# Chunk 3's probabilities transposed by VectorE and twelve transfers, with their values planned 1.5 units behind the scores

## The chip, the core and the metric

The kernel runs on one core of one Trainium2 chip. The metric is the device time of one execution in microseconds; lower is better. The engines that matter are TensorE (PE in the rows: matmuls, and matrix transposes through an identity), VectorE (DVE), ScalarE (ACT), GpSimd (POOL) and SyncE (SP), which here only issues transfers (DMAs). Each engine works through its own list of instructions in order.

## The reference

Two stages: windowed attention (8 batches, 8 heads, 576 positions, head size 64), then a feed-forward block on 4608 tokens of width 512.

```python
def _attn_ref(q, k, v):
    scores = scale * np.matmul(q, k.transpose(0, 1, 3, 2))
    mask = (rel >= 0) & (rel < 64)          # rel = query position - key position
    scores = np.where(mask, scores, -1e9)
    attn = np.exp(scores - np.max(scores, axis=-1, keepdims=True))
    attn = attn / (np.sum(attn, axis=-1, keepdims=True) + 1e-09)
    return np.matmul(attn, v)

def _moe_ref(x, w_in, w_out):
    h = x @ w_in                             # 512 -> 2048
    sp = np.where(h > 20.0, h, np.log1p(np.exp(np.minimum(h, 20.0))))
    return (h * np.tanh(sp)) @ w_out         # 2048 -> 512
```

## The kernel before

The 4608 tokens are cut into 12 chunks of 384. For each chunk the attention gives `x` (as a high part `xh` and a low part `xl`), and the feed-forward block then runs over 16 blocks `f` of the hidden width. One step of it is `ffn_in` (12 matmuls into `h_ps`; L223 to L238 then work on the result with VectorE, ScalarE and GpSimd) and `flush` (9 matmuls into the three accumulators `acc`, of the step two back). In the rows a step of the steady state is therefore twelve `h_ps` matmuls and nine `acc` matmuls.

The attention of a chunk is done in 4 pairs of heads (`p` = 0 to 3), while the feed-forward block of the chunk before it runs: chunk 3's attention lies inside chunk 2's feed-forward block. A pair has three parts. `scores` is 24 small matmuls into `s_ps`; then six reductions (L150), six exponentials (L153) and the normalisation (L161 to L163) give the probabilities `pr`; the loads of `q_t` and `k_t` for the pair two later follow on SP. `transpose` turns `pr` into `pT`. `values` is 24 small matmuls into `o_ps` (from `pT` and `v_t`), the copies to `xh` and `xl` (L205, L206), and on SP the load of `v_t` for the pair two later, which waits until this pair's values are through TensorE, since there are two buffers.

`transpose` exists in two forms. Up to chunk 3: six TensorE transposes into PSUM tiles `t_ps` (L184), then two copies from there into `pT` (L185, one on ScalarE, one on VectorE). From chunk 4 on: one VectorE transpose of 32x32 blocks into `tr` (L173), then twelve transfers of 24 KB (L178), all issued by SP, which put the blocks at their places in `pT`. The first matmul of `values` waits for all twelve. I call the twelve a train below. `tr` takes its buffers from the same two that `pr` uses.

What runs when is planned in half-steps, called slots here: slot 2n follows the n-th `ffn_in`, slot 2n+1 the n-th `flush`. `plan` (L320) places pair p's scores at begin + p·step, its transpose 0.6·step later, its values lag·step later, with lag 1. For chunk 3, begin is 71 and the last values fall on 90, so that step is 19/4 = 4.75 slots; from chunk 4 on a step is 8 slots. A scheduler then orders VectorE's and ScalarE's instructions by its own estimate of times and by priorities; TensorE's order within the attention follows the plan.

Of the kernel before, what the change touches and what calls it, by code (L numbers as in the profile page):

```python
# [27 lines left out]
def tile_window_attn_mish_ffn(  # L28
# [11 lines left out]
    NPAIR, _, NT = qT.shape  # L40
# [65 lines left out]
    def bank(c, p, name):  # L106
        if c == 2 or (c == 0 and p % 2 == 0):
            return ps_acc.tile([P, CH], F32, name=name, tag=next(sums))
        return ps_at.tile([P, CH], F32, name=name, tag="at")
# [55 lines left out]

    def att_transpose(c, p, pr):
        pT = next(pTs)
        if c > 3:


            moved = []
            tr = ap_.tile([P, P // 32, HM, 32], F32, name="tr", tag="pr", bufs=2)
            nc.vector.transpose(tr.rearrange("p k j i -> p j k i"),  # L173
                                pr.rearrange("p j (k i) -> p j k i", i=32))
            for r in range(0, P, 32):
                for k in range(0, P, 32):
                    if 0 <= k - r % BLK <= BLK:
                        moved.append(nc.sync.dma_start(pT[k:k + 32, r // 32, :, :], tr[r:r + 32, k // 32, :, :]))  # L178
            return pT, moved
        for h in range(2):  # L180
            t_ps = (bank(c, p, "t_ps") if c else ps_h.tile([P, CH], F32, name="t_ps", tag="h_ps")
                    ).rearrange("p (m k) -> p m k", k=P)
            for m in range(NM):
                order.append(nc.tensor.transpose(t_ps[:, m, :], pr[:, h * NM + m, :], ident).ins)  # L184
            (nc.scalar.copy if h == 0 else nc.vector.tensor_copy)(  # L185
                pT[:, :, h * NM:(h + 1) * NM, :].rearrange("p r m i -> p m r i"),
                t_ps.rearrange("p m (r i) -> p m r i", i=32))
        return pT, []
# [101 lines left out]
    class Att:  # L290
# [18 lines left out]
        def transpose(self, p):  # L309
            with in_order():  # L310
                self.pT[p] = att_transpose(self.c, p, self.pr.pop(p))
# [55 lines left out]
    starts = {c: 2 * len(steps) + 2 * NF * (c - 2) for c in range(2, NCHUNK)}  # L367
    steps += [(c, f) for c in range(2, NCHUNK) for f in range(NF)]

    atts = [Att(c) for c in range(NCHUNK)]  # L370
# [20 lines left out]
    ahead = 6  # L391
    begin = starts[2] + ahead + 1
    for c in range(3, NCHUNK):
        atts[c].plan(begin, (starts[c] - ahead - begin) / NPAIR)
        begin = starts[c] - ahead
    events.sort(key=lambda e: e[:2])
    ordered.append(True)
# [52 lines left out]
```

## Time and profile before

| | us |
|---|---|
| median of 3 runs (964.61 to 969.32) | 967.43 |
| the profiled execution | 967.45 |
| its span, first to last instruction | 965.6 |
| TensorE busy | 918.2 |
| VectorE busy | 489.0 |
| ScalarE busy | 624.5 |
| GpSimd busy | 330.4 |

The profiled execution's time is 1.85 us above its span, and within 0.1 us of the median. The rows of the next sections come from that execution; times in them are microseconds from the start of its span. The timeline gives the start of an instruction and its duration, merges equal neighbours (x24), and shows in brackets how long its engine had been idle before and what ended that. The chain of waits that ended last gives, in order of time, which work the end of the kernel hung on.

### The profile page before, as it was taken

What the parts mean: (1) busy time and instruction counts of PE and PEld (TensorE: products, weight loads), DVE (VectorE), ACT (ScalarE), POOL (GpSimd) and SP (SyncE); (2) the same over time, 40 slices, a digit from 0 to 9 for tenths busy, and PEclk for the clock granted to TensorE, in tenths of its full rate; (3) what the DMA queues carried; (4) which work ended last, traced back from release to release, by engine and by line L of the source; (5) the groups of instructions that cost most, each with busy time, mean ns of one, the idle gap of its engine ahead of it and who ended that gap; (6) DMA issues with size and microseconds to landing.
All of it is one profiled execution on the core that took longest, in us unless ns stands there. A gap on an engine that the chain in (4) does not pass through costs nothing.

```text
span 965.6 us, 18005 instructions
## 1 busy us (share of the span) xinstructions
PE 918.2 (95%) x6432; PEld 813.7 (84%) x6432; DVE 489.0 (51%) x1352; ACT 624.5 (65%) x1529; POOL 330.4 (34%) x419
## 2 busy tenths in 40 slices
PE   4667989999999999999999999999999999999997
PEld 3556878888888888888988898889888898889996
DVE  6799884353455445545444544544454544452222
ACT  5677676675666666666666665766756666665664
POOL 2253554223323333233333333333323333333333
PEclk9679999999999999999999999999999999999999
DMA  7645430131123223222222311311312322200000
GB/s 247 193 165 192 136 107 1 51 98 55 52 70 102 65 54 85 80 57 78 85 56 63 100 54 54 114 52 54 114 51 56 104 59 56 89 24 13 33 1 34
DMA packets 80345, 76.16 MB, mean 79 GB/s; under 512 B 9600, under 2 KB 71552, under 8 KB 80256
## 3 DMA queue, kind: packets, MB, share of 16 engines
q1 hardware_dynamic: 80256, 75.01, 25.5%
q8 instruction: 51, 0.84, 0.4%
q14 instruction: 38, 0.31, 0.1%
HBM read 56.10 MB, written 9.44 MB: 68 GB/s over the span
## 4 chain that ended last, share of the span: by engine, by line
PE 83%; DVE 6%; issue 3%; ACT 3%; DMA 3%; POOL 1%; SPq 1%; ACTq 0%; POOLq 0%; DVEq 0%
PE h_ps L96 38%; PE acc L96 37%; PE o_ps L96 4%; PE s_ps L96 3%; DMA st<-w_out 2%; DVE wa L277 1%; DVE wa L278 1%; ACT wa L273 1%; SPq L178 1%; POOL wo_l L280 1%; ACT pr L153 1%; DVE wi_l L280 1%; PE t_ps L184 1%; DVE pr L150 0%; DVE wa L276 0%
## 5 line engine op out<-in xcount | busy, mean ns | idle before, releaser
L224 ACT ACTIVATE t<-t 128x384 f32<-128x384 f32 x192 | 100.7, 524 | 266.1 <-DVE t L223 265.7
L237 POOL TENSOR_SCALAR gh<-t 128x384 fp32r<-128x384 f32 x176 | 91.3, 519 | 518.1 <-DVE t L233 498.3
L96 PE MATMUL h_ps<-xh,wi_h 128*128 128x384 f32 x768 | 261.6, 341 | 3.3 <-DVE t L233 3.2
L96 PE MATMUL h_ps<-xh,wi_l 128*128 128x384 f32 x768 | 259.4, 338 | 0.0
L96 PE MATMUL h_ps<-xl,wi_h 128*128 128x384 f32 x768 | 259.2, 337 | 0.0
L96 PE MATMUL acc<-wo_h,gh 128*128 128x512 f32 x576 | 231.0, 401 | 0.5 <-POOL gh L237 0.5
L96 PE MATMUL acc<-wo_l,gh 128*128 128x512 f32 x576 | 226.6, 393 | 0.0
L233 DVE SCALAR_TENSOR_TENSOR t<-t,h_ps 128x384 f32<-128x384 f32 x176 | 97.3, 553 | 245.6 <-ACT t L231 240.7
L238 POOL TENSOR_TENSOR gl<-t,gh 128x384 fp32r<-128x384 f32 x192 | 199.0, 1036 | 38.6 <-ACT gh L235 24.0
L96 PE MATMUL acc<-wo_h,gl 128*128 128x512 f32 x576 | 205.5, 393 | 0.0
L96 PEld LDWEIGHTS h_ps<-xh,wi_h 128*128 128x128 f32 x768 | 145.3, 189 | 13.5 <-DVE t L233 5.4
L96 PEld LDWEIGHTS h_ps<-xl,wi_h 128*128 128x128 f32 x768 | 145.3, 189 | 6.7
L96 PEld LDWEIGHTS h_ps<-xh,wi_l 128*128 128x128 f32 x768 | 145.4, 189 | 0.0
L223 DVE TENSOR_SCALAR t<-h_ps 128x384 f32<-128x384 f32 x192 | 106.5, 555 | 68.3 <-PE h_ps L96 64.8
L96 PEld LDWEIGHTS acc<-wo_h,gh 128*128 128x128 f32 x576 | 109.0, 189 | 24.1 <-issue 6.5
L96 PEld LDWEIGHTS acc<-wo_h,gl 128*128 128x128 f32 x576 | 108.7, 189 | 23.7 <-POOL gl L238 0.7
L96 PEld LDWEIGHTS acc<-wo_l,gh 128*128 128x128 f32 x576 | 109.0, 189 | 16.7 <-issue 0.2
L230 ACT ACTIVATE t<-t,half_b 128x384 f32<-128x384 f32 x192 | 118.3, 616 | 5.6
L229 ACT ACTIVATE t<-t,one_b 128x384 f32<-128x384 f32 x192 | 118.4, 616 | 4.2
L153 ACT ACTIVATE pr<-pr,mx 128x128 f32<-128x128 f32 x288 | 111.4, 389 | 8.5 <-DVE mx L150 8.5
L231 ACT ACTIVATE t<-t 128x384 f32<-128x384 f32 x192 | 100.2, 522 | 4.6
L150 DVE CUSTOM_DVE_ANT_0 pr<-s_ps,mask 128x128 f32<-128x128 f32 x288 | 64.4, 285 | 7.5 <-PE s_ps L96 7.5
(49 smaller groups left out, 668.1 us busy)
## 6 DMA issues: line engine op xcount, KB each, us to landing
v_t<-vN SPq DMA_DIRECT2D x48, 384.0 KB, 3.7
k_t<-kT SPq DMA_DIRECT2D x47, 224.0 KB, 3.8
out<-o SPq DMA_DIRECT2D x36, 256.0 KB, 2.3
pT<-tr SPq DMA_DIRECT2D x384, 24.0 KB, 1.8
q_t<-qT SPq DMA_DIRECT2D x47, 192.0 KB, 3.7
st<-w_in SPq DMA_DIRECT2D x16, 512.0 KB, 4.0
st<-w_out SPq DMA_DIRECT2D x16, 512.0 KB, 3.5
q_t<-qT SPq DMA_DIRECT2D x3, 64.0 KB, 2.0
```

What stands on the lines that cost most here:

```text
L96: order.append(nc.tensor.matmul(*args, **kw).ins)
L150: nc.vector.tensor_tensor_reduce(out=pr[:, j, :], in0=s_ps[h][:, m, :], in1=mk, op0=ALU.add, op1=ALU.min, scale=-0.125, scalar=3.0e38, acc ...
L153: nc.scalar.activation(pr[:, j, :], pr[:, j, :], AF.Exp, bias=mx[:, j:j + 1], scale=-1.0, accum_out=sm[:, j:j + 1])
L223: nc.vector.tensor_scalar(t, h_ps, 20.0, None, ALU.min)
L224: nc.scalar.activation(t, t, AF.Exp)
L229: nc.scalar.activation(t, t, AF.Square, bias=one_b)
L230: nc.scalar.activation(t, t, AF.Ln, bias=half_b, scale=0.5)
L231: nc.scalar.activation(t, t, AF.Exp, scale=-1.0)
L233: nc.vector.scalar_tensor_tensor(t, t, -1.0, h, ALU.add, ALU.mult)
L237: nc.gpsimd.tensor_scalar(gh, t, 1.0, 0.0, ALU.mult, ALU.add)
L238: nc.gpsimd.tensor_tensor(gl, t, gh.bitcast(F32), ALU.subtract)
L280: (nc.vector if first else nc.gpsimd).tensor_tensor(wl, af, wh.bitcast(F32), ALU.subtract)
```

## The change

Chunk 3 takes the second form of `transpose`. Its plan gets 1.5 units between scores and values, and the unit becomes 19/4.5 = 4.22 slots, so that the last values still fall on slot 90.

```diff
     def att_transpose(c, p, pr):
         pT = next(pTs)
-        if c > 3:
+        if c > 2:
...
     for c in range(3, NCHUNK):
-        atts[c].plan(begin, (starts[c] - ahead - begin) / NPAIR)
+        if c == 3:
+
+            atts[c].plan(begin, (starts[c] - ahead - begin) / (NPAIR + 0.5), lag=1.5)
+        else:
+            atts[c].plan(begin, (starts[c] - ahead - begin) / NPAIR)
         begin = starts[c] - ahead
```

Outside chunk 3's attention the order of instructions is the same on each engine, but for the place of one or two `acc` matmuls among their neighbours. Inside it, three things move.

On TensorE, at chunk 3's first pair, the values leave their place beside the second pair's scores (numbers behind names, as in `pT_106`, are buffers):

```order
@@ -831,5 +830,4 @@
 L96 MATMUL h_ps<-xl_1974,wi_h 128x384
 L96 MATMUL h_ps<-xh_1973,wi_l 128x384
-L96 MATMUL o_ps<-pT_106,v_t 64x64 x12
 L96 MATMUL s_ps<-k_t,q_t 64x128 x12
 L96 MATMUL acc_2376<-wo_h,gh 128x512
```

and come one step later, after the next twelve `h_ps` matmuls:

```order
@@ -854,4 +852,5 @@
 L96 MATMUL h_ps<-xl_1974,wi_h 128x384
 L96 MATMUL h_ps<-xh_1973,wi_l 128x384
+L96 MATMUL o_ps<-pT_106,v_t 64x64 x12
 L96 MATMUL acc_2376<-wo_h,gh 128x512
 L96 MATMUL acc_2376<-wo_l,gh 128x512
```

The second and third pair go the same way; only the fourth pair's values keep a neighbour, the first scores of chunk 4. With `S`, `V`, `h` and `a` for the scores, the values, twelve `h_ps` and nine `acc` matmuls, the row before was S0 h a h T0 a h V0 S1 a h a T1 h a V1 S2 h a h T2 a h V2 S3 a h a T3 h V3, and is now S0 h a h a h S1 a h V0 a h S2 a h V1 a h S3 a h V2 a h a h V3.

On SP, in chunk 3's attention, the loads stood alone before:

```order
L117 DMA q_t<-qT 128x384
L119 DMA k_t<-kT 128x448
L126 DMA v_t<-vN 128x6x128
L117 DMA q_t<-qT 128x384
L119 DMA k_t<-kT 128x448
L126 DMA v_t<-vN 128x6x128
```

and now have a train between them, the second pair's (into `pT_107`) behind the `v_t` load that waits for the first pair's values:

```order
L178 DMA pT_106<-tr 32x192 x12
L117 DMA q_t<-qT 128x384
L119 DMA k_t<-kT 128x448
L126 DMA v_t<-vN 128x6x128
L178 DMA pT_107<-tr 32x192 x12
L117 DMA q_t<-qT 128x384
L119 DMA k_t<-kT 128x448
```

On VectorE, at the second pair, the copy out of PSUM came behind the normalisation:

```order
L163 TENSOR_TENSOR pr<-pr,sm 128x768
L223 TENSOR_SCALAR t<-h_ps 128x384
L185 COPY pT_107<-t_ps 128x3x4x32
L233 SCALAR_TENSOR_TENSOR t<-t,h_ps 128x384
L223 TENSOR_SCALAR t<-h_ps 128x384
```

and the block transpose now stands two instructions behind it (for the first pair none lies between; for the third and fourth it is the same two):

```order
L161 TENSOR_SCALAR sm<-sm 128x6
L162 RECIPROCAL sm<-sm 128x6
L163 TENSOR_TENSOR pr<-pr,sm 128x768
L233 SCALAR_TENSOR_TENSOR t<-t,h_ps 128x384
L223 TENSOR_SCALAR t<-h_ps 128x384
L173 STREAM_TRANSPOSE tr<-pr 128x6x4x32
```

## Rows read from the trace of the kernel before

**Rows 1.** The page: span, TensorE's busy time, granted clock in 40 slices (tenths).

```profile
span 965.6 us, 18005 instructions
...
PE 918.2 (95%) x6432; PEld 813.7 (84%) x6432; DVE 489.0 (51%) x1352; ACT 624.5 (65%) x1529; POOL 330.4 (34%) x419
...
PEclk9679999999999999999999999999999999999999
```

**Rows 2.** The chain that ended last, chunk 3's attention: start, us, work.

```profile
222.17 0.85 PE o_ps L96 x24
223.01 2.28 PE h_ps L96 x12
...
239.75 0.82 PE s_ps L96 x24
240.56 2.29 PE h_ps L96 x12
242.85 2.05 PE acc L96 x9
244.90 2.08 PE h_ps L96 x12
246.98 0.66 PE t_ps L184 x6
247.64 2.08 PE acc L96 x9
...
251.80 0.85 PE o_ps L96 x24
252.65 0.82 PE s_ps L96 x24
253.46 2.27 PE acc L96 x9
```

**Rows 3.** VectorE's timeline, pair 0 of chunk 3 and pair 1 of chunk 4.

```profile
244.48 0.96 DVE L163 TENSOR_TENSOR pr<-pr,sm 128x768 f32<-128x768 f32 x1
...
314.08 0.55 DVE L223 TENSOR_SCALAR t<-h_ps 128x384 f32<-128x384 f32 x1
314.55 0.97 DVE L173 STREAM_TRANSPOSE tr<-pr 128x768 f32<-128x768 f32 x1
```

**Rows 4.** SP's timeline of transfers issued in chunks 4 and 6, and the page's landing time.

```profile
315.58 7.49 SPq L178 DMA_DIRECT2D pT<-tr  x12
...
326.08 0.39 SPq L126 DMA_DIRECT2D v_t<-vN  x1
...
544.44 0.59 SPq L178 DMA_DIRECT2D pT<-tr  x1
...
573.78 8.76 SPq L178 DMA_DIRECT2D pT<-tr  x12
...
pT<-tr SPq DMA_DIRECT2D x384, 24.0 KB, 1.8
```

**Rows 5.** TensorE's timeline: scores and values of that pair, and values that waited.

```profile
307.56 0.89 PE L96 MATMUL s_ps<-k_t,q_t 64*64 64x128 f32 x24
...
325.12 0.92 PE L96 MATMUL o_ps<-pT,v_t 128*64 128x64 f32 x24
...
546.75 0.92 PE L96 MATMUL o_ps<-pT,v_t 128*64 128x64 f32 x24 [0.60 <-DMA pT<-tr]
```

**Rows 6.** TensorE behind idle stretches; the stage row ends in granted clock, DMA share, GB/s.

```profile
22.37 0.48 PE L96 MATMUL o_ps<-pT,v_t 128*64 128x64 f32 x2 [2.39 <-ACT pT L185]
...
22.00:24.00 2.00, 1.63 (x26) 1.45 (x26) 2.00 (x7) 0.71 (x3) 0.00 (x0) 0.50 0.27 82
...
81.36 0.85 PE L184 MATMUL t_ps<-ident,pr 128*128 128x128 f32 x6 [1.36 <-ACT t L224]
...
96.96 0.78 PE L96 MATMUL acc<-wo_h,gh 128*128 128x512 f32 x1
...
100.85 0.92 PE L96 MATMUL o_ps<-pT,v_t 128*64 128x64 f32 x24
```

## The prediction

> **What bounds the kernel now.** I read the page first. TensorE is busy 918.2 of 965.6 us, no other engine over two thirds, and the granted clock stands at nine tenths or more from the fourth of the forty slices on [rows 1]. Then the chain of waits in the stretch that the change touches, 239 to 293 us: every piece of it is TensorE's, one block after another without a gap [rows 2]. So in this stretch a microsecond of work taken off TensorE is a microsecond of span, and a microsecond that TensorE has to wait is one too. Nothing later gives it back, because the stretch behind is bound in the same way. What VectorE and ScalarE gain or lose counts only where TensorE waits for them.
>
> **What leaves TensorE.** Six transposes take 0.66 us, and the block behind them at most 0.03 more (2.08 against 2.05 for nine `acc`) [rows 2]. Four pairs: 2.7 us less. The copies out of PSUM that go with them lie beside TensorE's work and are worth nothing.
>
> **What comes back on TensorE.** Small matmuls slow the block behind them. Alone, the scores cost 0.82 us and 0.21 on the next block (2.29 against 2.08), 1.03 in all; alone, the values cost 0.85 and 0.20 (2.28 against 2.08), 1.05. Side by side they cost 0.85 + 0.82 + 0.22 (2.27 against 2.05) = 1.89 [rows 2]. Parting them therefore costs 1.03 + 1.05 - 1.89 = 0.19 us, and the new order parts three pairs: 0.6 us. TensorE's own work thus falls by 2.7 - 0.6 = 2.1 us.
>
> **The new wait.** The values now wait for a train, so its length has to be found from the trace. SP needs 7.49 us to issue twelve transfers, 0.62 each, and they land 1.8 us after issue [rows 4]. Values that did wait for a train started 546.75 - 544.44 = 2.31 us after the start of its last issue [rows 4, 5]; the landing time alone would say 1.8. The last issue starts 7.49 - 0.59 = 6.9 us after the first. So values can start 8.7 to 9.2 us after SP begins the train, and I take 9.1, near the values that did wait. From chunk 4 on that fits, but only just: the train of 315.58 is ready at 324.7 and its values start at 325.12, 17.56 us after their scores at 307.56 [rows 4, 5].
>
> From the scores to the end of the VectorE transpose that same pair takes 314.55 + 0.97 - 307.56 = 7.96 us, with one instruction (L223) between normalisation and transpose [rows 3, 5]. In chunk 3 the first pair has none: normalised at 244.48 + 0.96, so transposed at 246.4. Pairs 1 to 3 have two, the second for 0.47 us more (314.08 to 314.55), less something, since VectorE also emptied an accumulator (L261) within that pair's 7.96 us, which it doesn't do here. I take 8.2 us, between 7.6 (pair 0's 6.7 and two instructions) and 8.4.
>
> Now pair by pair, with TensorE's blocks from above and the rest of the order taken as it stands, from the scores at 239.75 on:
> - Pair 0: without T0 the second scores start at 246.98 + 2.05 + 2.08 = 251.1 and the values are due at 251.1 + 1.03 + 2.05 + 2.08 = 256.3. Train ready: 246.4 + 9.1 = 255.5. No wait, 0.8 us to spare.
> - Pair 1: due 256.3 + 1.05 + 2.05 + 2.08 + 1.03 + 2.05 + 2.08 = 266.6. Ready 251.1 + 8.2 + 9.1 = 268.4. **Wait 1.8.**
> - Pair 2: here SP's queue decides. Its train stands behind the `v_t` load, which waits for pair 1's values: in the row of 326.08 that load is issued 0.96 us after the values start and takes 0.39 [rows 4, 5]. So the train begins 1.4 us after 268.4, at 269.8, and is ready at 278.9. Due 268.4 + 10.3 = 278.7. **Wait 0.2.** The transpose itself (done by 270) is not the last here. It also needs `tr` free, which pair 1's train gives back when it has landed, at about 268.1, before the transpose would start at 268.6.
> - Pair 3: its scores start at 268.4 + 1.05 + 2.05 + 2.08 = 273.6, so its train is ready at 273.6 + 8.2 + 9.1 = 290.9. Due, with no scores in between, 278.9 + 1.05 + 2 x (2.05 + 2.08) = 288.2. **Wait 2.7.**
>
> The waits come to 4.7 us. TensorE's list is in order, so the feed-forward block that is queued behind each waiting matmul waits with it; that is why a wait here is lost in full.
>
> **What costs nothing.** The VectorE transpose (0.97 us) in place of a copy is hidden by the same TensorE blocks. It can put off the release of an `h_ps` buffer behind it (L233) by about that much, but each buffer is wanted again only two `ffn_in` later, 2 x (2.05 + 2.08) = 8.3 us after it was begun. Without that cover it would be 0.97 us a pair. The loads of `q_t` and `k_t` that now stand behind a train are wanted ten or more us after they land. The new train of pair 3 is over on SP before the first train of chunk 4 is due.
>
> **Sum.** -2.1 + 4.7 = +2.6 us against the profiled execution's 967.45: 970.1 us, 0.3% more. With 7.6 and 8.7 instead of 8.2 and 9.1 the waits fall by 2.1 (to 0.8, 0 and 1.8), with 8.4 and 9.2 they rise by 0.7. One train as slow as that of 573.78 (8.76 against 7.49 [rows 4]; some 5 of the 32 trains are visibly longer than 7.6) adds 1.3. So this case spans 968 to 972.
>
> **Rivals.**
> (A) *The train is hidden and only the saving shows*: 967.45 - 2.1 = 965.3. This needs trains of at most about 4.8 us (7.49 less the longest wait, 2.7), or transposes that come as much sooner. For it speaks that in later chunks the values hardly ever wait. Against it, that their trains have 17.56 us from scores to values, while pair 1 here has 15.5 and pair 3 has 14.6. Most trains take 7.48 to 7.50. The Trainium skill (DMA: Bandwidth & Descriptors, section Issuing engines are not separate DMA queues) says that the sequencer's time to initiate a transfer is usually small relative to the transfer itself. By that rule a train would be ready little over one landing after its start, which is this rival's time; the trace doesn't agree, with 0.62 us for each issue against 1.8 us to landing, and twelve in a row.
>
> (B) *The wait costs the clock, and the kernel is slower beyond doubt.* After an idle stretch of 2.39 us early in the kernel TensorE worked at a granted clock of 0.50, that is 1.2 GHz; after one of 1.36 us six transposes still took 0.85 us, as at 2.4 GHz [rows 6]. At the low level nine `acc` matmuls took 100.85 - 96.96 = 3.9 us [rows 6] instead of 2.05, 1.8 us lost before the clock came back; with the work around them I count 2.2. Pair 3's wait of 2.7 us is the place, and it decides from somewhere between 1.4 and 2.4 us on. That gives 970.1 + 2.2 = 972.3, and with pair 1's wait as well 974.5. Against it: the early stretch lay among others (the engine was idle much of the time around it), while here TensorE works without a gap on both sides.
>
> **How the numbers follow.** The forecast, waits that outweigh the saving: 0.63. (A): 0.15. (B): 0.20. Something not thought of: 0.02. About 0.5%, 4.8 us, is what a measurement of this kernel can tell from no change: below 962.6 is faster, above 972.3 slower. Faster: even (A) doesn't reach it, 0.03. Slower: most of (B) and a slow train or two, 0.19. Within 0.5%: 0.78. The range goes down to (A), 965.0, and up to (B) with one loss of clock and some more, 973.2; left out are (B) twice over and gains beyond (A).
>
> **What would show it.** In the trace of the changed kernel: no `t_ps` from 240 us on; four trains of about 7.5 us on SP between 246 and 290 us; first pair's values without a wait; idle time of TensorE ended by the transfer to `pT` of about 1.8, 0.2 and 2.7 us before the second, third and fourth values; the fourth at about 291 us; a `v_t` load at the head of the third train; granted clock 1.00 through the stretch. The prediction is wrong if a train of twelve takes markedly less than 7.5 us here, if the transposes come over a microsecond sooner than 8.2 us after the scores, or if the clock falls after pair 3's wait.

## The result and the profile after

The changed kernel takes 970.68 us (median of 16 runs, 968.40 to 974.51) against 967.48 for the kernel before (16 runs): ratio 1.0036, 95% interval 1.0026 to 1.0046. It is slower by 3.2 us, small but clear of zero. The profiled execution took 968.54 us with a span of 966.8, which is among the shortest of the runs; a possible reason for part of the spread comes out below.

The page of the kernel after, against [rows 1]: TensorE has 2.6 us less to do, and yet the span is 1.2 us longer.

```profile
span 966.8 us, 18025 instructions
...
PE 915.6 (95%) x6408; PEld 809.9 (84%) x6408; DVE 489.0 (51%) x1352; ACT 623.4 (64%) x1525; POOL 331.6 (34%) x419
...
PEclk9779999999999999999999999999999999999999
```

TensorE's timeline in chunk 3's attention, its scores and values alone (start, us, work; idle time before it and what ended it in brackets):

```profile
238.77 0.89 PE L96 MATMUL s_ps<-k_t,q_t 64*64 64x128 f32 x24
250.14 0.89 PE L96 MATMUL s_ps<-k_t,q_t 64*64 64x128 f32 x24
255.32 0.92 PE L96 MATMUL o_ps<-pT,v_t 128*64 128x64 f32 x24
260.52 0.89 PE L96 MATMUL s_ps<-k_t,q_t 64*64 64x128 f32 x24
267.05 0.92 PE L96 MATMUL o_ps<-pT,v_t 128*64 128x64 f32 x24 [1.27 <-DMA pT<-tr]
272.24 0.89 PE L96 MATMUL s_ps<-k_t,q_t 64*64 64x128 f32 x24
278.39 0.92 PE L96 MATMUL o_ps<-pT,v_t 128*64 128x64 f32 x24 [0.90 <-DMA pT<-tr]
...
289.47 0.92 PE L96 MATMUL o_ps<-pT,v_t 128*64 128x64 f32 x24 [1.69 <-DMA pT<-tr]
```

The first pair's values start without a wait; those of pairs 1, 2 and 3 wait for the transfer into `pT`, 3.9 us in all. The chain of [rows 2], which was TensorE's alone, now runs through SP's issues here and, from the last issue of each of these trains, through its landing (start, us, what):

```profile
265.12 1.84 DMA pT<-tr
...
276.46 1.79 DMA pT<-tr
...
287.39 1.80 DMA pT<-tr
```

A last transfer lands 1.8 us after its issue began, as in the kernel before [rows 4], and the values start 0.1 to 0.3 us after that. SP's trains in the same stretch, and the load between them:

```profile
245.61 8.05 SPq L178 DMA_DIRECT2D pT<-tr  x12
...
258.22 7.48 SPq L178 DMA_DIRECT2D pT<-tr  x12
...
267.99 0.38 SPq L126 DMA_DIRECT2D v_t<-vN  x1
268.56 8.49 SPq L178 DMA_DIRECT2D pT<-tr  x12
...
280.27 7.71 SPq L178 DMA_DIRECT2D pT<-tr  x12
```

And VectorE's block transposes that they wait for:

```profile
257.19 0.97 DVE L173 STREAM_TRANSPOSE tr<-pr 128x768 f32<-128x768 f32 x1
...
267.56 0.97 DVE L173 STREAM_TRANSPOSE tr<-pr 128x768 f32<-128x768 f32 x1
...
279.28 0.97 DVE L173 STREAM_TRANSPOSE tr<-pr 128x768 f32<-128x768 f32 x1
```

Values start 8.83 us after the first issue of a train of 7.48 us (267.05 - 258.22), 9.83 after that of 8.49 and 9.20 after that of 7.71: each time 1.3 to 1.5 us after the train's end.

To compare executions I use the distance from chunk 3's first scores to its last values, since the time of those first scores varies by a microsecond or more from run to run (the first scores start at 238.77 here and at 239.68 in the profile of before). Before, the last values started at 288.29: 48.61 us. After: 289.47 - 238.77 = 50.70 us. The stretch is 2.1 us longer.

### The profile page after: what moved, and what is told of

It reads as the page before. It is cut to its first block, busy times and chain, and to the rows that moved or that the text cites. A ratio compares the mean times of both kernels' runs of the same rounds, so it can differ in the third digit from the quotient of the medians.

```text
span 966.8 us, 18025 instructions
## 1 busy us (share of the span) xinstructions
PE 915.6 (95%) x6408; PEld 809.9 (84%) x6408; DVE 489.0 (51%) x1352; ACT 623.4 (64%) x1525; POOL 331.6 (34%) x419
## 4 chain that ended last, share of the span: by engine, by line
PE 80%; DVE 6%; DMA 3%; SPq 3%; issue 3%; ACT 3%; POOL 2%; ACTq 0%; POOLq 0%; DVEq 0%
PE h_ps L96 36%; PE acc L96 36%; PE o_ps L96 3%; PE s_ps L96 3%; SPq L178 3%; DMA st<-w_out 2%; DVE wa L277 1%; ACT pr L153 1%; DVE wa L278 1%; DMA st<-w_in 1%; ACT wa L273 1%; POOL wo_l L280 1%; DMA pT<-tr 1%; POOL gl L238 1%; DVE t L233 0%
```

## The experiments

Four theories stood against each other. Theory 1: TensorE waits for the trains, that is for the time SP needs to issue twelve transfers. Rival 2: the new order costs the time. Rival 3: it is the VectorE transpose, or the landing of the transfers, and not their issue. And the prediction's rival (B): a wait brings the clock down.

**The plan alone** (e1). Its edit, and those of the experiments behind e2, are against the changed kernel:

```diff
-        if c > 2:
+        if c > 3:
```

> The new plan alone: chunk 3 keeps its TensorE transposes, values 1.5 units behind the scores. Theory 1 (the loss is TensorE waiting for trains of twelve issues): no train, so no wait; three pairs of scores and values are parted (0.19 us each), two transposes now stand beside values; 0.2 to 0.6 us slower than before, ratio about 1.0004, no idle time of TensorE between 240 and 292 us. Rival 2 (the new order itself costs the time): 2 to 3.5 us slower, as the full change.

Measured: 967.26 us against 966.81, ratio 1.0010 (1.0001 to 1.0019). First scores to last values: 288.27 - 238.50 = 49.77 us, 1.16 more than before. TensorE's waits in the stretch:

```profile
PE t_ps L184 <- DVE pr L163: 0.5, 2, 0.2
```

So 0.5 us are two transposes that now come a little before their `pr` is ready, which I hadn't foreseen, and some 0.7 us are the parted pairs, against 0.6 in the prediction. Rival 2 falls as the main cause: the order alone costs 1.2 us by the rows (0.1 to 1.8 by the ratio's interval), not the 2 to 3.5 that it would have to.

**The form alone** (e2), this one edit against the kernel before, whose plan stays:

```diff
-        if c > 3:
+        if c > 2:
```

> The new form of transpose alone: chunk 3 goes through the VectorE transpose and twelve transfers, values one unit behind the scores as before. Theory 1: each of the four values waits for its train, by about 4.4, 5.7, 5.7 and 7.8 us less half a us each (the trains were ready 8.9 us after their start in the changed kernel, not 9.1): 21 to 23 us of waiting less 2.7 us of transposes, 18 to 21 us slower, 986 to 988 us. If idle stretches of 4 us and more bring the clock down, 2.2 us for each on top, up to 997. Rival 2 (the order costs the time, and it is nearly the old one here): within 1 us of the kernel before or up to 2.7 us faster.

Measured: 987.11 us against 966.81, ratio 1.0214 (1.0199 to 1.0229). All four values wait, for 15.5 us by the profile:

```profile
254.45 1.55 PE L96 MATMUL o_ps<-pT,v_t 128*64 128x64 f32 x24 [4.37 <-DMA pT<-tr]
255.93 1.56 PE L96 MATMUL s_ps<-k_t,q_t 64*64 64x128 f32 x24
...
271.62 0.92 PE L96 MATMUL o_ps<-pT,v_t 128*64 128x64 f32 x24 [2.71 <-DMA pT<-tr]
272.47 1.09 PE L96 MATMUL s_ps<-k_t,q_t 64*64 64x128 f32 x24
...
289.00 0.92 PE L96 MATMUL o_ps<-pT,v_t 128*64 128x64 f32 x24 [3.55 <-DMA pT<-tr]
289.85 1.39 PE L96 MATMUL s_ps<-k_t,q_t 64*64 64x128 f32 x24
...
305.67 1.55 PE L96 MATMUL o_ps<-pT,v_t 128*64 128x64 f32 x24 [4.87 <-DMA pT<-tr]
```

The size is what theory 1 gave without the clock (18 to 21 us), though not by the same terms: the waits are shorter than the 21 to 23 us expected, and the clock makes up for it. They are shorter in part because the transposes come sooner: the second train begins at 262.80, 6.87 us after its scores, where the changed kernel needs 258.22 - 250.14 = 8.08. Behind waits of 4.4 and 4.9 us the values take 1.55 us instead of 0.92, and behind those of 2.7 and 3.6 us the clock falls a little later, in the scores (1.09 and 1.39 instead of 0.89). The stages around the first two waits (us, busy time of TensorE, weight loads, VectorE, ScalarE and GpSimd, then granted clock, DMA share, GB/s):

```profile
252.00:256.00 4.00, 1.55 (x28) 1.47 (x31) 0.56 (x1) 1.12 (x2) 1.52 (x2) 0.57 0.09 23
256.00:260.00 4.00, 4.00 (x31) 3.17 (x32) 1.91 (x13) 2.61 (x12) 0.00 (x0) 0.58 0.66 193
...
272.00:276.00 4.00, 4.00 (x51) 3.61 (x47) 1.86 (x13) 2.55 (x12) 0.28 (x1) 0.63 0.47 119
```

**Half a train** (e3). The transfers of source rows 64 to 127 are left out in chunk 3, so that half of the blocks of `pT` keep old contents there:

```diff
-                    if 0 <= k - r % BLK <= BLK:
+                    if 0 <= k - r % BLK <= BLK and (c > 3 or r < BLK):
```

> The changed kernel with six of chunk 3's twelve transfers left out (those of source rows 64 to 127, so half of the blocks of pT keep old contents); VectorE's transposes, the order and the plan stay. Theory 1: SP issues six in 3.8 us, the values can start 5.2 us after the first, no wait is left, and the saving of 2.1 us shows alone: 965.4, ratio 0.998. Rival 2 (order): 2 to 3.5 us slower than before. Rival 3 (what counts is the VectorE transpose or how long a transfer takes to land, not the number of issues): waits stay over 1 us, 0 to 3 us slower than before.

Measured: 964.38 us against 966.81, ratio 0.9976 (0.9967 to 0.9985). SP is done after 3.7 us, and no value waits:

```profile
259.33 3.69 SPq L178 DMA_DIRECT2D pT<-tr  x6
...
266.82 0.92 PE L96 MATMUL o_ps<-pT,v_t 128*64 128x64 f32 x24
...
286.53 0.92 PE L96 MATMUL o_ps<-pT,v_t 128*64 128x64 f32 x24
```

First scores (239.88) to last values: 46.65 us, 1.96 less than before. This is the saving of the prediction (2.1 us) with nothing in front of it, and it shows that VectorE's transposes and the landing of a transfer do no harm by themselves: rival 3 falls as far as these are meant. It halves both the issues and the bytes. That it is the issues follows with the rows of the changed kernel: each last transfer lands in 1.8 us as before, so what is left of the 8.8 us and more from first issue to values is the time to issue; and between 262.00 and 265.40, inside a train and clear of other loads, the DMA engines are busy for a share of 0.17, so bandwidth is not what a train lacks. A run with fewer issues for the same bytes wasn't made. Against this run's stretch, the changed kernel's waits come to 50.70 - 46.65 = 4.05 us.

**ScalarE issues half** (e6):

```diff
-                        moved.append(nc.sync.dma_start(...))
+                        moved.append((nc.scalar if c == 3 and r >= BLK else nc.sync).dma_start(...))
```

> The changed kernel with the six transfers of source rows 64 to 127 of chunk 3's trains issued by ScalarE instead of SP; bytes, number and order on TensorE stay. Theory 1 (the time to issue on one queue is what the values wait for): SP is done after 3.8 us, no wait on SP's half is left; ScalarE has 4 x 3.8 = 15 us more to do in 51, of which it was busy 34; if that stays off TensorE the saving of 2.1 to 2.4 us shows, 964.6 to 965.5; if ScalarE's part of the train or its activations come late, waits of a microsecond or two come back, up to 968. Rival 3 (the number of transfers in flight or their landing counts, whoever issues them): waits as in the changed kernel, 3 us slower than before.

Measured: 974.65 us against 966.89, ratio 1.0082 (1.0067 to 1.0097), outside what either theory gave. SP's half took 3.7 to 5.0 us, but the values of pairs 2 and 3 waited 3.7 and 3.3 us, and the clock fell behind both waits (1.42 and 1.55 us instead of 0.92):

```profile
279.98 1.42 PE L96 MATMUL o_ps<-pT,v_t 128*64 128x64 f32 x24 [3.66 <-DMA k_t<-kT]
...
294.24 1.55 PE L96 MATMUL o_ps<-pT,v_t 128*64 128x64 f32 x24 [3.33 <-DMA pT<-tr]
```

The first thing to come late here is the transpose:

```profile
272.19 0.97 DVE L173 STREAM_TRANSPOSE tr<-pr 128x768 f32<-128x768 f32 x1
...
283.14 0.97 DVE L173 STREAM_TRANSPOSE tr<-pr 128x768 f32<-128x768 f32 x1
```

It ends 12.5 and 13.0 us after the scores of these pairs (260.69 and 271.07), where the changed kernel needs 8.0. With the new issues ScalarE's list has another order: pair 2's first exponential starts 6.4 us after the scores (267.07), behind an activation that waited for VectorE, against 1.9 us in the changed kernel. At pair 2 ScalarE's own six issues are then over in 4.7 us (273.19 to 277.90), sooner than SP's twelve would be; the wait there is the late transpose's. At pair 3 the issues also stand between activations that wait for other engines. The first and the last of the six:

```profile
284.14 0.52 ACTq L178 DMA_DIRECT2D pT<-tr  x1
...
292.21 0.57 ACTq L178 DMA_DIRECT2D pT<-tr  x1
```

They are spread over 8.6 us, longer than SP needs for twelve. An issue of half a microsecond is cheap on ScalarE, but its place behind waiting work is not, and neither is what it does to the order of the work around it. As a test between issue and landing it decides nothing.

**Lag 2** (e5):

```diff
-            atts[c].plan(begin, (starts[c] - ahead - begin) / (NPAIR + 0.5), lag=1.5)
+            atts[c].plan(begin, (starts[c] - ahead - begin) / (NPAIR + 1), lag=2)
```

> The changed kernel with values two units behind scores and a unit of 19/5 = 3.8 slots; the order on TensorE becomes one in which two of the three parted pairs stand together again, VectorE's transposes follow the normalisation directly, and the train of pair 2 no longer stands behind the load that waits for pair 1's values. Theory 1: from scores to due values 16.8 to 17.6 us, trains ready 15.7 to 17 us after the scores, so waits of 0 to 0.5 us in all; TensorE's work 2.5 us less than before: 965 to 966, ratio 0.998 to 0.999. Rival 2 (order or dense attention costs the time): 1 us or more slower than before.

Measured: 966.62 us against 966.81, ratio 0.9997 (0.9984 to 1.0010): no loss, and no gain that can be told. One wait is left, 1.75 us at pair 3, where 0 to 0.5 us in all were expected. Part of it is something that I had set down as harmless in the prediction, and that cost nothing in the changed kernel: `tr` shares two buffers with `pr`. With scores 9.3 to 10.1 us apart a train is not landed when the next transpose wants the buffer, and VectorE waits before the transposes of pairs 1 to 3:

```profile
258.49 0.98 DVE L173 STREAM_TRANSPOSE tr<-pr 128x768 f32<-128x768 f32 x1 [1.54 <-DMA pT<-tr]
...
269.00 0.98 DVE L173 STREAM_TRANSPOSE tr<-pr 128x768 f32<-128x768 f32 x1 [1.07 <-DMA pT<-tr]
...
278.93 0.98 DVE L173 STREAM_TRANSPOSE tr<-pr 128x768 f32<-128x768 f32 x1 [0.49 <-DMA pT<-tr]
...
289.79 0.92 PE L96 MATMUL o_ps<-pT,v_t 128*64 128x64 f32 x24 [1.75 <-DMA pT<-tr]
```

Of pair 3's 1.75 us, 0.5 are this buffer, 1.0 a train with a slow issue (first issue at 279.94, values 9.85 us later instead of 8.83), and the rest is the plan. Transpose, train and landing, one after another, are 1.0 + 7.5 + 1.4 us and more where a train has a slow issue: by this sum, with scores closer than some 10 us a transpose waits for the train before it.

**Lag 1.75, last values on slot 92** (e7), which allows for both:

```diff
-            atts[c].plan(begin, (starts[c] - ahead - begin) / (NPAIR + 0.5), lag=1.5)
+            atts[c].plan(begin, (starts[c] - ahead + 2 - begin) / (NPAIR + 0.75), lag=1.75)
```

> A version meant to hide the trains: the changed kernel with values 1.75 units behind scores, a unit of 21/4.75 = 4.42 slots and the last values two slots later (92 instead of 90). From scores to due values 18.6 us for pairs 1 to 3, against some 17 us that transpose and train need, and scores at least 10.3 us apart, about what one train after another needs. Theory 1: no wait, all four values parted from scores, 2.7 - 0.8 = 1.9 us faster than before, ratio 0.998. If trains with slow issues or the wait for the buffer of tr come in, up to 1 us of that is lost. Rival 2 (order): slower than before by 1 us or more.

Measured: 964.92 us against 966.89, ratio 0.9985 (0.9973 to 0.9998). TensorE waits for no transfer anywhere in chunk 3, though three of its four trains took 8.5 us and more. From chunk 3's first scores to chunk 4's first values it takes 65.23 us (238.18 to 303.41), the kernel before 67.03 (239.68 to 306.71): 1.8 us less, near the 1.9 that were expected. The medians differ by 2.0 us, the ratio gives 1.5 with an interval from 0.2 to 2.6. So this version is faster than the changed kernel beyond doubt, and than the kernel before by little more than the noise.

**The changed kernel twice more** (e8, e9):

> The changed kernel once more, for the spread of its waits from run to run: theory 1 expects three waits before the values of pairs 1 to 3, 3.5 to 5 us in all, more where a train of chunk 3 has slow issues (over 7.6 us), and the granted clock at 1.00 behind them.

> As the run before, a second look: three waits, 3.5 to 5 us in all, the sum going with the length of the trains.

Measured: 970.27 and 971.61 us; three waits each for a transfer, 4.2 and 4.3 us in all. The first pair's values, too, come 0.2 and 0.3 us later behind the second scores than in the first profile (5.39 and 5.46 us, against 5.18), 1.4 us after the end of trains of 8.52 and 8.58 us. The last values of the one, and of the other with the scores behind them:

```profile
291.23 0.92 PE L96 MATMUL o_ps<-pT,v_t 128*64 128x64 f32 x24 [2.16 <-DMA pT<-tr]
```

```profile
291.30 1.26 PE L96 MATMUL o_ps<-pT,v_t 128*64 128x64 f32 x24 [2.58 <-DMA pT<-tr]
292.49 1.56 PE L96 MATMUL s_ps<-k_t,q_t 64*64 64x128 f32 x24
```

Behind the wait of 2.58 us in e9 came what rival (B) describes: the granted clock fell to its lower level (0.50). In e8, behind 2.16 us, it stayed at 1.00, as it did in the changed kernel's first profile. The same stage in e8 and in e9:

```profile
292.00:294.00 2.00, 2.00 (x34) 1.58 (x31) 1.82 (x9) 1.13 (x5) 1.02 (x2) 1.00 0.18 53
...
292.00:294.00 2.00, 2.00 (x36) 1.55 (x32) 0.94 (x2) 0.48 (x1) 1.38 (x2) 0.50 0.12 35
```

From the first scores to the last values e9 takes 51.45 us and e8 51.24; e9's loss of clock comes behind that. From there to the first values of chunk 4 e8 takes 18.42 us (291.23 to 309.65) and e9 19.94 (291.30 to 311.24): the clock costs 1.5 us. So the loss of the changed kernel isn't one number: against e3's stretch the waits cost 4.1 us in the first profile, 4.6 in e8 and 4.8 in e9, where pair 3's trains took 7.71, 8.24 and 8.46 us, and in e9 the clock adds its 1.5 us (in the whole it took 1.3 us more than e8). Part of the spread of 968.4 to 974.5 may come from there, and the first profile, with 1.69 us at pair 3, is one of the shorter. How many of the 16 runs lost the clock can't be told, since only these three were profiled.

## Why the prediction was right, and where its steps were off

The forecast was 970.1 us, the measurement 970.68. By its steps:

- **What leaves TensorE** (2.7 us) and **what comes back** (0.6): e3 shows the net as 1.96 against 2.1, e1 the second term as about 0.7. Right.
- **From the scores to the end of the transpose**: 8.2 forecast; 8.02, 8.01 and 8.01 measured (257.19 + 0.97 - 250.14 and so on). Right, 0.2 long.
- **From a train's first issue to its values**: 9.1 forecast; 8.83 for a train without a slow issue, up to 9.83 with one. Right on average. I had it from the one wait of [rows 5], 2.31 us from the last issue's start, where 1.9 is usual (8.83 - 6.9), and this happened to stand for the slow issues: luck.
- **Pair 0**: no wait, right. **Pair 1**: 1.8 forecast, 1.27 measured: the two terms above, 0.2 + 0.3 us.
- **Pair 2**: 0.2 forecast, 0.90 measured, and the step's reason was wrong. I had SP's queue decide, since its `v_t` load waits for pair 1's values. That load was through at 268.37, the transpose only at 268.53, and the train began at 268.56: with pair 1's wait shorter, the transpose was last by 0.2 us. The wait itself came from a slow issue (a train of 8.49 us; with 8.83 us to its values there would have been none), which I had only in the range.
- **Pair 3**: 2.7 forecast, 1.69 measured. The step failed in that I took its scores and pair 2's wait as I had forecast them. Pair 2's values stand between pair 3's scores and its own values, so 0.7 us more of waiting there is 0.7 us less here. The two waits together were 2.6 us against 2.9.
- **The sum of waits**: 4.7 forecast, 3.9 in the first profile, 4.2 and 4.3 in the others. That the total comes so close is in part luck: pairs 1 and 3 were put too long, pair 2 too short, and the slow issues and the clock, which the 4.7 does not name, happened to make up for it. The profiled execution lost 1.1 us of time (968.54 against 967.45) where 2.6 were forecast: the stretch itself lost 2.1, and the start of the kernel happened to be 0.9 shorter (238.77 against 239.68 at the first scores).
- **Rival (A)**, the hidden train: wrong here, since a train does take 7.5 us and not much less; but the plan was short of it by no more than the waits, 1.3 and 1.7 us, and e7's values, 19.7 us behind their scores instead of due after 15.6, wait for nothing.
- **Rival (B)**, the clock: it had 0.20 as another outcome, and proved to be a part of this one. One of three profiles shows it, e9, which meets one of the prediction's own signs of being wrong, a clock that falls after pair 3's wait. Its point was given as somewhere between 1.4 and 2.4 us; here the clock stayed up behind 2.16 us (e8) and fell behind 2.58 (e9) and 2.71 (e2). Its price was given as 2.2 us; in e9 it was 1.5. That the median lies 0.6 us above the forecast fits with it, but isn't shown.
- **What can be told from no change**: 0.5% forecast. With 16 runs of each kernel the interval is 0.2% wide, and a loss of 0.36% is clear.

## What to carry to other kernels

Where a step is moved from a busy engine to a chain of transfers, cost the chain by its issues: twelve small transfers on one queue took 7.5 us to issue before the last could land, and the plan has to hold the consumer back by the whole chain, here some 17 us from the scores through transpose, train and landing to the values, and has to leave time for the chain's own buffer to come free. A gain of 2 us was turned into a loss of 3 by some 4 to 5 us of waiting and, in one of three profiles, the clock, and moving the consumers 4 us later brought the gain back; measure both halves of such a change alone, as each was misleading by itself (about 1 us and 20 us slower). And on a bound TensorE a wait may cost the clock too: here every wait of 2.58 us and more in the experiments' stretch was followed by the lower clock, and none of up to 2.16 us.

## What was not expected of the hardware

One issue in a train sometimes takes 1.0 to 1.6 us where the others take 0.59 us. In chunk 3 this struck two trains of the first profile clearly (8.05 and 8.49 us), and three of four in e8, in e9, in e7 and in e5, while of the 32 trains of later chunks some five were visibly longer than 7.6 us. It is not tied to these transfers: in the profile of before, loads of `q_t` and `k_t` in the same stretch took 0.98 and 1.13 us to issue where the others took 0.3 to 0.4.

```profile
266.40 0.98 SPq L117 DMA_DIRECT2D q_t<-qT  x1
...
279.69 1.13 SPq L119 DMA_DIRECT2D k_t<-kT  x1
```

The traces show what goes with a slow issue. The page lists, beside the queue of the loads and transfers, a queue 8 of kind instruction, with 51 packets of 16 KB in an execution. In the changed kernel's first profile one of them falls in the train of 245.61 (8.05 us) and one in that of 268.56 (8.49 us), and none in that of 258.22 (7.48 us). The queue's row for 245.6 to 253.7 and for 268.5 to 277.1 (packets, MB, share of 16 engines):

```profile
q8 instruction: 1, 0.02, 0.7%
...
q8 instruction: 1, 0.02, 0.8%
```

Over all profiles but e6, 237 trains of twelve have no such packet begun in them or in the 0.9 us ahead of them, and none of these trains takes over 7.72 us; all 58 trains longer than 7.8 us have one. So the slow issues go with the loading of instructions, and in the changed kernel they meet the same trains each time: the second train has no such packet in any of its three profiles. Whose instructions these are, and whether the loading is the cause, wasn't tried and stays open.
